# Queries of batches 1 to 3 loaded once and doubled by GpSimd, and outputs of batch 0 turned by DMA in two fp16 parts

## The chip, the core and the metric

One core of a Trainium2 chip runs the whole program. The metric is device time in microseconds, the median of three runs. The engines are named as in the profile: PE (TensorE; PEld is its weight load), DVE (VectorE), ACT (ScalarE), POOL (GpSimd) and SP (SyncE, which only issues DMAs here). Memory on the core is SBUF, with 128 partitions, and PSUM, into which PE writes.

## What is computed

```python
# q, k, v: (4 batches, 8 heads, 768, 64) f32; blocks of 32 rows, 24 of them
scores = q @ k.T / 8        # kept where |block_i - block_j| <= 1, in the first and last
                            # block row or column, or in 3 sampled blocks per row
attn = softmax(where(mask, scores, -1e9))
x = (attn @ v)              # heads side by side: (3072 tokens, 512)
out = ((x @ w_a) * (x @ w_b)) @ w_out       # w_a, w_b 512 x 1536, w_out 1536 x 512
```

## The kernel before

Queries go by **chunks** of 256 rows: 3 per batch, 12 in all, in the order 1, 0, 2, 3, ... 11. A chunk has 8 **units** (one block row of 32 queries, all 8 heads). For each unit GpSimd copies the keys it needs side by side (`KG`, lines 731 to 740), SP gathers the values from memory (`VG`, lines 821 to 835), PE makes scores (`s`), ACT the exponentials (`sm`), and PE the products with the values (`av`). Two units share one bank of `av`; `output` divides both by their sums (tile `xs`), turns them so that features lie on partitions, and writes them as two fp16 parts, high and low, to `xT`. Four such pairs make the chunk's `xT`, on which the feed-forward layer runs: 12 steps of 24 matmuls `ab` (line 1497), a product (`g`, lines 1513 and 1516), and the matmuls `o` (lines 1581 to 1583).

Batch 0 is computed in f32 straight from the inputs. Its pairs (12 of them) are turned on PE by two f32 matmuls with a unit matrix (line 1448), and ACT and DVE read the turned sums from PSUM and write the two parts (lines 1459 and 1460). Batches 1 to 3 run in two fp16 parts everywhere; their pairs (36) are split in SBUF (tile `xo`, lines 1433 and 1434) and turned by a transposing DMA that SP issues (line 1436).

The queries of batches 1 to 3 (9 chunks) come with both halves of the partitions holding the same 64 features, since the contraction runs over the keys' high part on one half and their low part on the other. The array in memory holds them twice. `queries` loads a chunk in two halves of 4 heads (line 865, 512 KB each, issued by POOL) into one buffer `rq` of 4 KB per partition; `half_queries` takes the largest absolute value (ACT, line 895), makes a scale from it (`set_scale`: one reduction over partitions on POOL, line 447, and three short DVE instructions), and writes the high part (ACT, line 901) and the low part (DVE, line 902). The second half's load waits until the first half's low part is done.

During the first third of the program the weights arrive as 64-bit words (36 tiles of 512 KB, line 951), are put together by DVE (lines 972 to 978), scaled and split by ACT and DVE (lines 992 to 1000).

The order of the instructions on each engine is worked out before the program runs: `Plan.run` takes generators ("flows"), each of which yields an engine, a duration in ns and a function that issues the instruction, and issues next the one that could begin first by its estimate, with the flow's rank to decide between equals. Each engine then runs its list in order. `LEAD_Q` sets the rank of the query flows; `GATE_Q` is how many units ahead of a chunk its queries may be asked for, and the two buffers `QT` must be free too. `LATE_...` is added to an estimated landing before the work that reads the data may be planned: 2500 ns (`LATE_XT`) for the turned outputs of batches 1 to 3.

Of the kernel before, what the change touches and what calls it, by code (L numbers as in the profile page):

```python
# [46 lines left out]
PT_BUFS = 3  # L47
SM_BUFS = 3
LATE = 16
RAW_PLACES = 2  # L50
EVEN = 0
AT_ONCE = 4
# [17 lines left out]

LEAD_K = 6
LEAD_V = 5
LEAD_Q = 4
LEAD_X = -1
LEAD_G = 2
GATE_KV = 10
GATE_Q = 9
GATE_Q0 = 6
GATE_G = 3
R_W = 12  # L80
# [186 lines left out]
def pe(ns, fn):  # L267
    return [Way("PE", ns, fn)]


def dve(ns, fn):
    return [Way("DVE", ns, fn)]


def act(ns, fn):
    return [Way("ACT", ns, fn)]
# [11 lines left out]
def pool_load(moved, fn):  # L288

    return [Way("POOL", 1000, fn, moved, 1000)]  # L290
# [7 lines left out]
def kernel(  # L298
# [43 lines left out]
    def take(tag, bufs):  # L342
        return rings.setdefault(tag, Ring(bufs)).take()
# [507 lines left out]
    def queries(cc):  # L851

        b, c = divmod(cc, NCH)
        u0 = order[b, c * PER]
        yield from gate(u0 - (GATE_Q if b else GATE_Q0))
        if b == 0:
            yield from plain_queries(cc, u0)
            return
        q_used[cc] = yield from take("QT", QT_BUFS)
        QT[cc] = work.tile([P, 2, H, CH], F16, tag="QT", name=f"QT{cc}", bufs=QT_BUFS)  # L860
        known = Event(2)
        for half in range(2):
            freed = yield from take("rq", 1)
            t = work.tile([P, NG, CH], F32, tag="rq", name=f"q{cc}_{half}", bufs=1)
            end = yield pool_load(2000, lambda t=t, half=half: nc.gpsimd.dma_start(
                t, q[b, c, :, half * NG : (half + 1) * NG]
            ))
            plan.start(half_queries(cc, half, t, freed, known), u0 - LEAD_Q, end + LATE_LOAD)
        next_queries(cc)
        yield k_scale[b]  # L870
        yield known

        def factor():

            for i in range(2):
                ps = slice(i * 64, (i + 1) * 64)
                nc.vector.scalar_tensor_tensor(
                    cq[ps, cc, :],
                    rscale[ps, at_k + b * NG : at_k + (b + 1) * NG].rearrange(
                        "p (a i) -> p a i", i=2  # L880
                    )[:, :, i],
                    float(D) ** -0.5, rscale[ps, at_q + 2 * cc : at_q + 2 * cc + 2],
                    ALU.mult, ALU.mult,
                )

        end = yield dve(450, factor)
        q_ready[cc].fire(end)

    def half_queries(cc, half, t, freed, known):
        b, c = divmod(cc, NCH)  # L890
        u0 = order[b, c * PER]
        at = at_q + 2 * cc + half
        heads = slice(half * NG, (half + 1) * NG)
        high, low_ = QT[cc][:, 0, heads], QT[cc][:, 1, heads]
        yield act(1230, lambda: nc.scalar.activation(
            high, t, AF.Abs, accum_out=bound[:, at : at + 1]
        ))
        end = yield from set_scale(slice(at, at + 1), FLOOR_QK)
        known.fire(end)
        s = scale[:, at : at + 1]  # L900
        yield act(1120, lambda: nc.scalar.activation(high, t, AF.Copy, scale=s))
        end = yield dve(1250, lambda: nc.vector.scalar_tensor_tensor(
            low_, t, s, high, ALU.mult, ALU.subtract
        ))
        freed.fire(end)
        q_ready[cc].fire(end)

    def next_queries(cc):
# [492 lines left out]
    def output(b, i, bank, read):  # L1401

        cc = b * NCH + i // PER
        p = place[cc]
        if p >= X_BUFS:
            yield ffn_done[seq[p - X_BUFS]]
        to = xT[p % X_BUFS][:, i % PER // 2]
        at = order[b, i] % LATE
        xs = work.tile([P, 2, HQ, D], F32, tag="xs", name=f"xs{b}_{i}", bufs=XS_BUFS)
        held = yield from take("xs", XS_BUFS)  # L1410
        dn = den[:, at : at + 2, :, 0]
        over = dn.unsqueeze(3).to_broadcast([P, 2, HQ, D])
        if b == 0:
            yield dve(165, lambda: nc.vector.tensor_scalar(dn, dn, EPS, None, ALU.add))
        else:
            yield v_scale[b]
            yield dve(165, lambda: nc.vector.scalar_tensor_tensor(
                dn, dn, EPS, evened[:, b].unsqueeze(1).to_broadcast([P, 2, HQ]),
                ALU.add, ALU.mult,
            ))  # L1420
        yield dve(160, lambda: nc.vector.reciprocal(dn, dn))
        sums = bank.rearrange("p y (i a d) -> p y i a d", i=2, a=HQ)
        if b == 0:
            yield dve(418, lambda: nc.vector.tensor_mul(xs, sums[:, 0], over))
        else:
            yield act(470, lambda: nc.scalar.copy(xs, sums[:, 1]))
            t = yield dve(418, lambda: nc.vector.tensor_add(xs, xs, sums[:, 0]))
            read.fire(t + LATE_AV)
            yield dve(430, lambda: nc.vector.tensor_mul(xs, xs, over))
            gone = yield from take("xo", XO_BUFS)  # L1430
            xo = work.tile([P, 2, 2, P], F16, tag="xo", name=f"xo{b}_{i}", bufs=XO_BUFS)
            flat = xs.rearrange("p i a d -> p i (a d)")
            yield act(400, lambda: nc.scalar.copy(xo[:, 0], flat))
            t = yield dve(420, lambda: nc.vector.tensor_sub(xo[:, 1], flat, xo[:, 0]))
            held.fire(t)
            t = yield sp(900, 760, lambda: nc.sync.dma_start_transpose(
                to.rearrange("p a x k q -> p (a x) (k q)"), xo.rearrange("p a i c -> p (a i c)")
            ))
            gone.fire(t + LATE_XO)
            x_ready[cc].fire(t + LATE_XT)  # L1440
            x_ready[cc].fire(t + LATE_XT)
            return
        ps = bank[:, 1].rearrange("p (i c) -> p i c", i=2)
        yield LATE_X if b else LATE_X0

        def turns_():
            for x in range(2):
                nc.tensor.transpose(
                    ps[:, x], xs[:, x].rearrange("p a d -> p (a d)"), eye
                )  # L1450

        t = yield pe(280, turns_)
        held.fire(t)
        if b == 0:
            yield v_scale[0]
        s = scale[:, at_v : at_v + 1] if b == 0 else 1.0
        of = ps.rearrange("p i c -> p (i c)")
        hi, lo = (to[:, a].rearrange("p x k q -> p (x k q)") for a in range(2))
        yield act(470, lambda: nc.scalar.activation(hi, of, AF.Copy, scale=s))
        t = yield dve(420, lambda: nc.vector.scalar_tensor_tensor(  # L1460
            lo, of, s, hi, ALU.mult, ALU.subtract
        ))
        read.fire(t + (LATE_AV if b else 0))
        x_ready[cc].fire(t)
        x_ready[cc].fire(t)


    gates, g_free = {}, {}
# [254 lines left out]
```

## Time and profile before

| | |
|---|---|
| median of 3 runs | 802.25 us (799.92 to 805.12) |
| the profiled execution's own time | 809.73 us |
| its span, first to last instruction | 807.6 us |
| granted PE clock, mean over the span | 0.976 |
| PE, PEld busy | 739.6 us (92%), 529.0 us (66%) |
| DVE, ACT, POOL busy | 522.0 us (65%), 492.0 us (61%), 228.4 us (28%) |
| DMA, whole span | 133.76 MB, 166 GB/s |

Busy time counts instructions that run; an engine that stands in front of a wait is idle. "DMA share" is the mean busy share of the core's 16 DMA engines. The clock is 1.00 at PE's upper level.

### The profile page before, as it was taken

Reading aid. Unit: us, or ns where it says so; the run is one execution under the profiler, and the core shown is the slowest. Engines: PE = TensorE matmul, PEld = TensorE weight load, DVE = VectorE, ACT = ScalarE, POOL = GpSimd, SP = SyncE. Lnnn points to the kernel's source line nnn. Section 1 sums busy time; section 2 is a strip of 40 time slices with the busy share of each in tenths; the row PEclk is TensorE's granted clock in tenths of the full one; section 3 lists DMA queues with packets and bytes.
Section 4 is the critical chain, followed back from the end, with each engine's and each line's share of the span. In section 5 each row is a group of like instructions: output and inputs, shape, how many; then the busy total and the mean of one; then the engine's idle time right before and its main releaser. Section 6 shows DMA issues by size and latency. Waiting matters only on the chain.

```text
span 807.6 us, 25925 instructions
## 1 busy us (share of the span) xinstructions
PE 739.6 (92%) x10056; PEld 529.0 (66%) x10056; DVE 522.0 (65%) x1478; ACT 492.0 (61%) x1226; POOL 228.4 (28%) x542
## 2 busy tenths in 40 slices
PE   2759979989989999899799999899899999999997
PEld 0426757864568767648568768558478768678853
DVE  4699979876766767575667676665666675622132
ACT  2767878875655776566556686666457565533333
POOL 4728743213233342121133332221133220000001
PEclk9968999999999999999999999999899999999999
DMA  9898667767687999885686799996688567630001
GB/s 271 239 285 246 204 212 241 217 126 178 146 181 164 198 139 224 184 208 144 154 177 170 167 194 194 184 241 133 147 180 175 137 141 148 137 83 1 2 0 53
DMA packets 185318, 133.76 MB, mean 166 GB/s; under 512 B 135851, under 2 KB 155948, under 8 KB 185196
## 3 DMA queue, kind: packets, MB, share of 16 engines
q1 hardware_dynamic: 172044, 84.85, 51.6%
q0 software_dynamic: 11616, 44.05, 18.1%
q10 hardware_dynamic: 1536, 3.21, 1.2%
q8 instruction: 79, 1.29, 0.7%
q14 instruction: 43, 0.35, 0.1%
HBM read 89.59 MB, written 11.01 MB: 125 GB/s over the span
## 4 chain that ended last, share of the span: by engine, by line
PE 69%; DMA 12%; DVE 8%; ACT 5%; issue 4%; SPq 1%; POOL 1%; POOLq 1%; ACTq 0%; DVEq 0%
PE ab L1497 39%; PE o L1581 7%; PE o L1583 6%; PE o L1582 6%; PE av L1094 4%; PE s L1035 4%; DMA pt<-hl 4%; DMA VG<-in_v_dram 2%; DMA stage<-in_v_dram 1%; DMA vp<-in_v_dram 1%; DMA q<-in_q_dram 1%; DMA keysT<-in_moe_w_b_dram 1%; SPq L835 1%; DMA keysT<-in_k_dram 1%; DVE wab L1000 1%
## 5 line engine op out<-in xcount | busy, mean ns | idle before, releaser
L1497 PE MATMUL ab<-xT,wab 128*128 128x256 f16 x3456 | 393.7, 275 | 7.6 <-ACT pt L1147 4.4
L1497 PEld LDWEIGHTS <-wab 128*128 128x128 f16 x3456 | 336.4, 99 | 61.0 <-issue 15.3
L1516 DVE TENSOR_TENSOR g<-g,ab 128x256 f32<-128x256 f32 x144 | 60.4, 419 | 119.2 <-ACT g L1513 118.5
L1513 ACT ACTIVATE g<-ab,f 128x256 f32<-128x256 f32 x144 | 67.9, 472 | 100.3 <-PE ab L1497 99.6
L1550 ACT ACTIVATE gh<-g,scale 128x256 f16<-128x256 f32 x144 | 70.9, 505 | 81.1 <-PE o L1583 76.1
L1551 DVE SCALAR_TENSOR_TENSOR gh<-g,scale,gh 128x256 f16<-128x256 f32 x144 | 68.3, 485 | 72.9 <-ACT gh L1550 71.8
L1581 PE MATMUL o<-wo,gh 128*128 128x512 f16 x288 | 110.7, 384 | 1.8 <-ACT gh L1550 1.8
L1582 PE MATMUL o<-wo,gh 128*128 128x512 f16 x288 | 110.2, 383 | 0.0
L1583 PE MATMUL o<-wo,gh 128*128 128x512 f16 x288 | 110.2, 382 | 0.0
L731 POOL COPY KG<-keysT 128x384 int32<-128x384 int32 (+1 forms) x86 | 50.0, 582 | 171.6 <-PE s L1035 144.1
L740 POOL COPY KG<-keysT 128x128 int32 (+1 forms) x264 | 88.5, 373 | 34.2 <-POOL KG L731 23.3
L1198 ACT ACTIVATE sm<-s,low,cq 128x256 f32<-128x256 f32 x132 | 73.9, 563 | 27.2 <-DVE low L1192 16.5
L447 POOL PARTITION_ALL_REDUCE power<-bound x67 | 28.9, 432 | 201.3 <-DVE bound L1530 82.4
L1061 DVE SCALAR_TENSOR_TENSOR hl<-sm,hl 128x256 f16<-128x256 f32 (+1 forms) x156 | 68.9, 452 | 1.6
L1186 DVE TENSOR_REDUCE low<-s 128x2 f32<-128x512 f32 x88 | 59.8, 680 | 6.8 <-PE s L1035 4.8
L1094 PE MATMUL av<-VG,pt 128*32 128x64 f32 (+2 forms) x2160 | 42.2, 218 | 24.0 <-DMA pt<-hl 9.7
L1581 PEld LDWEIGHTS <-gh 128*128 128x128 f16 x288 | 28.3, 98 | 37.7 <-issue 5.0
L1583 PEld LDWEIGHTS <-gh 128*128 128x128 f16 x288 | 28.4, 98 | 34.9 <-issue 1.1
L1582 PEld LDWEIGHTS <-gh 128*128 128x128 f16 x288 | 28.4, 99 | 30.5 <-issue 1.1
L1094 PEld LDWEIGHTS <-pt 128*32 128x32 f16 x2032 | 26.5, 97 | 27.0 <-DMA pt<-hl 16.3
L1520 ACT ACTIVATE junk<-g 128x1024 f16<-128x1024 f32 x36 | 37.9, 1053 | 9.9 <-DVE g L1516 9.3
L1035 PE MATMUL s<-KG,QT 128*32 128x256 f16 x1056 | 40.3, 273 | 0.0
(142 smaller groups left out, 946.4 us busy)
## 6 DMA issues: line engine op xcount, KB each, us to landing
VG<-vd SPq DMA_DIRECT2D x147, 64.0 KB, 2.8
q<-in_q_dram POOLq DMA_DIRECT2D x18, 512.0 KB, 5.6
VG<-vd SPq DMA_DIRECT2D x45, 192.0 KB, 3.4
out_dram<-ou POOLq DMA_DIRECT2D x24, 256.0 KB, 4.3
VG<-vd SPq DMA_DIRECT2D x15, 384.0 KB, 3.7
stage<-in_v_dram POOLq DMA_DIRECT2D x12, 384.0 KB, 5.2
vd<-vs SPq DMA_DIRECT2D x12, 384.0 KB, 5.3
stage<-in_k_dram POOLq DMA_DIRECT2D x12, 384.0 KB, 5.6
```

Of the source, the lines that this page charges most:

```text
L740: nc.gpsimd.tensor_copy(to[:, :, (5 + r) * w : (6 + r) * w], of[:, :, bass.ds(at, w)])
L1035: mm(to[h * BLK : (h + 1) * BLK], q_block(cc, i, 4 * hq + h, a), rhs(4 * hq + h), start=(first and a == 0), stop=(a == 1), skip_group_chec ...
L1061: t = yield dve(221 + n * 1.03, lambda: nc.vector.scalar_tensor_tensor(lo, sm, over, hi, ALU.mult, ALU.subtract))
L1094: mm(both[hs, :, i % 2, hq] if two else av[hs, i % 2, hq], pt[:, y, hs], of if two or b == 0 else of[:, 0], start=(i % 2 == 0 and hq == 0 ...
L1198: t = yield act(750, lambda hq=hq: nc.scalar.activation(sm[:, hq], ps[:, hq], AF.Exp, bias=low[:, at, hq, 0:1], scale=factor_of(b, cc, hq) ...
L1497: mm(ab[:, i, :].rearrange("p (j x q) -> p j x q", j=PER // 2, x=2), wab[:, f, i, part, kt, :], xc[:, :, a, :, kt, :], start=(i == 0 and k ...
L1513: yield act(460, lambda: nc.scalar.activation(g, ab[:, 0, :], AF.Copy, scale=f1[:, f : f + 1]))
L1550: yield act(400, lambda: nc.scalar.activation(gh[:, 0], g, AF.Copy, scale=s))
L1551: t = yield dve(480, lambda: nc.vector.scalar_tensor_tensor(gh[:, 1], g, s, gh[:, 0], ALU.mult, ALU.subtract))
L1581: mm(po, gh[:, 0, js], wo[:, x, 0], start=(x == 0), stop=False)
L1582: mm(po, gh[:, 0, js], wo[:, x, 1], start=False, stop=False)
L1583: mm(po, gh[:, 1, js], wo[:, x, 0], start=False, stop=(x == NF - 1))
```

## The change

The constants first: `LATE_XT0 = 1000` is new, `LEAD_Q` goes from 4 to 6, `GATE_Q` from 9 to 12.

**Queries.** A chunk's buffer now holds the first 4 heads on partitions 0 to 63 and the last 4 on 64 to 127, so that two loads of 64 partitions bring each number once (256 KB each), one after the other and without a wait between them. One absolute maximum and one scale serve the whole chunk. High and low part are written for 64 partitions at a time, and then a GpSimd copy brings both parts of those 4 heads to the other half of the partitions.

**Outputs of batch 0.** The two matmuls with the unit matrix, and the reads from PSUM, go. The divided sums are split in SBUF with the values' scale, into `xo`, and turned by the same transposing DMA that batches 1 to 3 use; the bank of `av` is given back right after the division.

```diff
         q_used[cc] = yield from take("QT", QT_BUFS)
         QT[cc] = work.tile([P, 2, H, CH], F16, tag="QT", name=f"QT{cc}", bufs=QT_BUFS)
-        known = Event(2)
-        for half in range(2):
-            freed = yield from take("rq", 1)
-            t = work.tile([P, NG, CH], F32, tag="rq", name=f"q{cc}_{half}", bufs=1)
-            end = yield pool_load(2000, lambda t=t, half=half: nc.gpsimd.dma_start(
-                t, q[b, c, :, half * NG : (half + 1) * NG]
+        known = Event()
+        freed = yield from take("rq", 1)
+        t = work.tile([P, NG, CH], F32, tag="rq", name=f"q{cc}", bufs=1)
+        for y in range(2):
+            ps = slice(y * D, (y + 1) * D)
+            end = yield pool_load(1000, lambda ps=ps, y=y: nc.gpsimd.dma_start(
+                t[ps], q[b, c, ps, y * NG : (y + 1) * NG]
             ))
-            plan.start(half_queries(cc, half, t, freed, known), u0 - LEAD_Q, end + LATE_LOAD)
+        plan.start(split_queries(cc, t, freed, known), u0 - LEAD_Q, end + LATE_LOAD)
         next_queries(cc)
         yield k_scale[b]
         yield known
@@ -879,30 +881,50 @@
                     rscale[ps, at_k + b * NG : at_k + (b + 1) * NG].rearrange(
                         "p (a i) -> p a i", i=2
                     )[:, :, i],
-                    float(D) ** -0.5, rscale[ps, at_q + 2 * cc : at_q + 2 * cc + 2],
+                    float(D) ** -0.5, rscale[ps, at_q + 2 * cc : at_q + 2 * cc + 1].to_broadcast([64, HQ]),
                     ALU.mult, ALU.mult,
                 )
 
         end = yield dve(450, factor)
         q_ready[cc].fire(end)
 
-    def half_queries(cc, half, t, freed, known):
-        b, c = divmod(cc, NCH)
-        u0 = order[b, c * PER]
-        at = at_q + 2 * cc + half
-        heads = slice(half * NG, (half + 1) * NG)
-        high, low_ = QT[cc][:, 0, heads], QT[cc][:, 1, heads]
+    def split_queries(cc, t, freed, known):
+        at = at_q + 2 * cc
+        to = QT[cc]
         yield act(1230, lambda: nc.scalar.activation(
-            high, t, AF.Abs, accum_out=bound[:, at : at + 1]
+            to[:, 0, :NG], t, AF.Abs, accum_out=bound[:, at : at + 1]
         ))
         end = yield from set_scale(slice(at, at + 1), FLOOR_QK)
         known.fire(end)
-        s = scale[:, at : at + 1]
-        yield act(1120, lambda: nc.scalar.activation(high, t, AF.Copy, scale=s))
-        end = yield dve(1250, lambda: nc.vector.scalar_tensor_tensor(
-            low_, t, s, high, ALU.mult, ALU.subtract
-        ))
+
+        def part(y):
+            ps, heads = slice(y * D, (y + 1) * D), slice(y * NG, (y + 1) * NG)
+            return ps, to[ps, 0, heads], to[ps, 1, heads], scale[ps, at : at + 1]
+
+        def high(y):
+            ps, hi, lo, s = part(y)
+            nc.scalar.activation(hi, t[ps], AF.Copy, scale=s)
+
+        def low_(y):
+            ps, hi, lo, s = part(y)
+            nc.vector.scalar_tensor_tensor(lo, t[ps], s, hi, ALU.mult, ALU.subtract)
+
+        def other(y):
+            ps, heads = slice(y * D, (y + 1) * D), slice(y * NG, (y + 1) * NG)
+            qs = slice((1 - y) * D, (2 - y) * D)
+            nc.gpsimd.tensor_copy(
+                to[qs, :, heads].rearrange("p a h q -> p a (h q)").bitcast(I32),
+                to[ps, :, heads].rearrange("p a h q -> p a (h q)").bitcast(I32),
+            )
+
+        for y in range(2):
+            yield act(1120, lambda y=y: high(y))
+            end = yield dve(1250, lambda y=y: low_(y))
+            plan.start(doubled(cc, lambda y=y: other(y)), order[cc // NCH, cc % NCH * PER] - LEAD_Q, end)
         freed.fire(end)
+
+    def doubled(cc, fn):
+        end = yield pool(1350, fn)
         q_ready[cc].fire(end)
 
     def next_queries(cc):
```

```diff
         yield dve(160, lambda: nc.vector.reciprocal(dn, dn))
         sums = bank.rearrange("p y (i a d) -> p y i a d", i=2, a=HQ)
         if b == 0:
-            yield dve(418, lambda: nc.vector.tensor_mul(xs, sums[:, 0], over))
+            t = yield dve(418, lambda: nc.vector.tensor_mul(xs, sums[:, 0], over))
+            read.fire(t)
         else:
             yield act(470, lambda: nc.scalar.copy(xs, sums[:, 1]))
             t = yield dve(418, lambda: nc.vector.tensor_add(xs, xs, sums[:, 0]))
             read.fire(t + LATE_AV)
             yield dve(430, lambda: nc.vector.tensor_mul(xs, xs, over))
-            gone = yield from take("xo", XO_BUFS)
-            xo = work.tile([P, 2, 2, P], F16, tag="xo", name=f"xo{b}_{i}", bufs=XO_BUFS)
-            flat = xs.rearrange("p i a d -> p i (a d)")
+        gone = yield from take("xo", XO_BUFS)
+        xo = work.tile([P, 2, 2, P], F16, tag="xo", name=f"xo{b}_{i}", bufs=XO_BUFS)
+        flat = xs.rearrange("p i a d -> p i (a d)")
+        if b == 0:
+            yield v_scale[0]
+            s = scale[:, at_v : at_v + 1]
+            yield act(400, lambda: nc.scalar.activation(xo[:, 0], flat, AF.Copy, scale=s))
+            t = yield dve(480, lambda: nc.vector.scalar_tensor_tensor(
+                xo[:, 1], flat, s, xo[:, 0], ALU.mult, ALU.subtract
+            ))
+        else:
             yield act(400, lambda: nc.scalar.copy(xo[:, 0], flat))
             t = yield dve(420, lambda: nc.vector.tensor_sub(xo[:, 1], flat, xo[:, 0]))
-            held.fire(t)
-            t = yield sp(900, 760, lambda: nc.sync.dma_start_transpose(
-                to.rearrange("p a x k q -> p (a x) (k q)"), xo.rearrange("p a i c -> p (a i c)")
-            ))
-            gone.fire(t + LATE_XO)
-            x_ready[cc].fire(t + LATE_XT)
-            x_ready[cc].fire(t + LATE_XT)
-            return
-        ps = bank[:, 1].rearrange("p (i c) -> p i c", i=2)
-        yield LATE_X if b else LATE_X0
-
-        def turns_():
-            for x in range(2):
-                nc.tensor.transpose(
-                    ps[:, x], xs[:, x].rearrange("p a d -> p (a d)"), eye
-                )
-
-        t = yield pe(280, turns_)
         held.fire(t)
-        if b == 0:
-            yield v_scale[0]
-        s = scale[:, at_v : at_v + 1] if b == 0 else 1.0
-        of = ps.rearrange("p i c -> p (i c)")
-        hi, lo = (to[:, a].rearrange("p x k q -> p (x k q)") for a in range(2))
-        yield act(470, lambda: nc.scalar.activation(hi, of, AF.Copy, scale=s))
-        t = yield dve(420, lambda: nc.vector.scalar_tensor_tensor(
-            lo, of, s, hi, ALU.mult, ALU.subtract
-        ))
-        read.fire(t + (LATE_AV if b else 0))
-        x_ready[cc].fire(t)
-        x_ready[cc].fire(t)
+        t = yield sp(900, 760, lambda: nc.sync.dma_start_transpose(
+            to.rearrange("p a x k q -> p (a x) (k q)"), xo.rearrange("p a i c -> p (a i c)")
+        ))
+        gone.fire(t + LATE_XO)
+        late = LATE_XT if b else LATE_XT0
+        x_ready[cc].fire(t + late)
+        x_ready[cc].fire(t + late)
 
 
     gates, g_free = {}, {}
```

## Rows read from the trace of the kernel before

**Rows 1.** The page, part 1: busy us, share, instructions.
```profile
PE 739.6 (92%) x10056; PEld 529.0 (66%) x10056; DVE 522.0 (65%) x1478; ACT 492.0 (61%) x1226; POOL 228.4 (28%) x542
```
**Rows 2.** Stretches: start:end, length, busy us per engine, clock, DMA.
```profile
core 0: us, PE busy (x) PEld busy (x) DVE busy (x) ACT busy (x) POOL busy (x), PEclk, DMA share, GB/s
20.00:60.00 40.00, 26.91 (x420) 14.76 (x421) 31.68 (x75) 27.05 (x86) 19.77 (x43) 0.82 0.94 263
60.00:116.00 56.00, 50.06 (x848) 36.68 (x848) 54.31 (x130) 46.34 (x132) 38.27 (x70) 0.95 0.76 229
116.00:720.00 604.00, 575.92 (x8135) 415.94 (x8135) 405.17 (x1185) 383.48 (x943) 158.62 (x399) 0.99 0.79 172
300.00:350.00 50.00, 44.35 (x622) 33.00 (x614) 31.34 (x96) 30.79 (x72) 10.24 (x29) 0.97 0.99 199
500.00:550.00 50.00, 46.31 (x612) 31.55 (x610) 33.58 (x104) 31.25 (x72) 10.88 (x28) 1.00 0.94 189
```
**Rows 3.** Chain that ended last: start us, us, what.
```profile
101.05 8.13 DMA keysT<-in_moe_w_b_dram
...
116.32 4.45 PE ab L1497 x24
...
180.21 1.04 ACT QT L895 x2
```
**Rows 4.** Waits of TensorE: total us, times, longest.
```profile
PE av L1094 <- DMA pt<-hl: 13.2, 9, 3.3
...
PE av L1094 <- ACT pt L1147: 7.3, 5, 2.5
...
PE av L1094 <- DMA VG<-in_v_dram: 6.0, 5, 1.9
```
**Rows 5.** Stretches, line 1448 alone; and their sum.
```profile
0.00:60.00 60.00, 1.51 (x6) 0.74 (x6) 0.88 0.93 266
...
116.00:808.00 692.00, 1.58 (x8) 0.95 (x8) 0.99 0.70 152
sum 808.00, PE 5.11 PEld 2.84; mean PE 1.70 PEld 0.95
```
**Rows 6.** Timeline of TensorE: start, us, what.
```profile
68.17 0.38 PE L1448 MATMUL av<-eye,xs 128*128 128x128 f32 x2
...
68.48 0.54 PE L1094 MATMUL av<-vp,pt 128*32 128x64 f32 x24
...
71.99 2.79 PE L1497 MATMUL ab<-xT,wab 128*128 128x256 f16 x24
```
**Rows 7.** Tile xo: ns min/median/max, first and last start.
```profile
L1434 DVE TENSOR_TENSOR xo<-xs,xo x36: 410/419/724, 226.2 to 723.4; 128x256 f16<-128x256 f32 x36
L1436 SPq DMA_TRANSPOSE xT<-xo x36: 1188/1207/2937, 228.5 to 723.9; - x36
...
DMA to landing us min/median/max: 2.4/4.0/7.2
```
**Rows 8.** The page, part 3: queue, packets, MB, share.
```profile
q1 hardware_dynamic: 172044, 84.85, 51.6%
q0 software_dynamic: 11616, 44.05, 18.1%
```
**Rows 9.** Tile QT: ns min/median/max.
```profile
L895 ACT ACTIVATE QT<-q x18: 1039/1049/1061, 111.7 to 617.9; 128x1024 f16<-128x1024 f32 x18
L895 ACT ACTIVATION_READ_ACCUMULATOR QT<-q x18: 185/190/205, 112.6 to 618.9; 128x1 f32 x18
L902 DVE SCALAR_TENSOR_TENSOR QT<-q,scale,QT x18: 1254/1283/1378, 134.0 to 626.8; 128x1024 f16<-128x1024 f32 x18
```
**Rows 10.** GpSimd by line: ns min/median/max; its longest wait.
```profile
L731 POOL COPY KG<-keysT x86: 498/511/1522, 14.7 to 672.7; 128x384 int32<-128x384 int32 x66, 128x384 f32<-128x384 f32 x20
L740 POOL COPY KG<-keysT x264: 288/297/1509, 11.7 to 674.4; 128x128 int32 x99, 128x128 f32 x33
...
POOL KG L731 <- PE s L1035: 144.1, 34, 14.2
```

More of the change, by code (lines that the diff above doesn't have):

```diff
@@ L49 @@
 LATE = 16
+LATE_XT0 = 1000
 RAW_PLACES = 2
@@ L72 @@
 LEAD_V = 5
-LEAD_Q = 4
+LEAD_Q = 6
 LEAD_X = -1
@@ L76 @@
 GATE_KV = 10
-GATE_Q = 9
+GATE_Q = 12
 GATE_Q0 = 6
```

## The prediction

> **What bounds the kernel now.** I read the page's busy times first. PE is at work for 739.6 of 807.6 us, no other engine for more than 65% [rows 1], so what is taken from another engine counts only where PE stands still for it. The stretches say where that is. In 60 to 116 us DVE is busy for 54.31 of 56 us while PE has 50.06 and a clock of 0.95; from 116 to 720 us PE has 575.92 of 604 us at 0.99 and no other engine is above 68% [rows 2]. The chain of waits agrees: it passes through the weights' arrival at 101.05 us and the first stretch of feed-forward matmuls after it at 116.32 us [rows 3]. So there are three regimes. Up to 60 us memory sets the pace (DMA share 0.94 in 20 to 60 us), up to 116 us it is DVE's unpacking of weights, and then PE, which up to 720 us stands still for 604 - 575.92 = 28.1 us in all. That is all that better feeding of PE could win there; beyond it only PE's own work can shrink. The waits name the largest piece of it: 13.2 us in front of the products with the values, for the turned exponentials' DMA [rows 4]. Two stretches hold much of the rest: 300 to 350 us (5.65 us idle, DMA share 0.99) and 500 to 550 us (3.69 us, 0.94) [rows 2].
>
> **Turns off PE.** 24 matmuls with their weight loads go, 5.11 us of PE in all [rows 5]. Those before 116 us win nothing by themselves: PE was not the bound there. The 8 after it (4 pairs) are 1.58 us busy. A pair really takes 68.48 - 68.17 = 0.31 us of PE's time, as the next matmul shows [rows 6]. So 4 x 0.31 = 1.2 us, on the path: **-1.2 us**. Ends: 0 (a stall behind takes it up) and -5.1 (all 24 count).
>
> **The parts of batch 0's outputs.** The 12 ACT and 12 DVE instructions that write the parts stay in number; DVE's takes 0.419 us in later batches [rows 7]. Both its inputs are now in SBUF; the longest such case took 0.724 us [rows 7], so at most 12 x 0.305 = 3.7 us more of DVE. Of the 12 pairs 3 fall before 60 and 4 after 116 us [rows 5], so 5 lie in DVE's own stretch: 1.5 us if every one is held. I take 0, the median's case, and keep 0 and +3.7 as ends.
>
> **The turn by DMA.** Added: 12 transposing DMAs on SP, 1.2 us of issue each, landing 2.4 to 7.2 us after it, 4.0 in the median [rows 7]. This takes the place of a 0.31 us turn. Chunk 1's last turn was at 68.17 us and its first feed-forward step at 71.99 us [rows 6]; the split was in between anyway, so the data now come later by 4.0 - 0.3 = 3.7 us in the median and 6.9 us at worst. PE has units of attention to do meanwhile, if the written order puts them first: the order counts with 1 us after its own estimate of the landing (2.5 us for later batches), so it knows most of this. I take **+1 us**, for one of three chunks a third of the median; ends 0 and +11 (three chunks by 3.7). The transposes wait on SP for DVE's low part; behind them on SP are the gathers of values, for which PE waits: 6.0 us in five places already, in the memory-bound start [rows 4]. A transpose is 131 KB. Queue q1 took 0.516 x 807.6 = 417 us for 84.85 MB [rows 8], 4.9 us per MB, so 0.64 us each, 7.7 us of DMA time for 12. The 3 pairs before 60 us make 1.9 us there; half of it on the path: **+1 us**, ends 0 and +3.6 (3 x 1.2 us of SP).
>
> **Queries.** Bytes: 18 loads of 0.524 MB become 18 of half that, 4.72 MB less. Queue q0 took 0.181 x 807.6 = 146 us for 44.05 MB [rows 8], 3.3 us per MB: 15.6 us of DMA time less, against 7.7 us more above. In the two full stretches (300 to 350 and 500 to 550 us) one load each of 0.524 x 3.3 = 1.7 us less lies in front of what PE waits for: **-3.5 us**. Ends: 0 (the loads were hidden) and -13.2 (the whole wait).
> ACT: 9 times 1.049 + 0.190 us less [rows 9], 11.2 us. ACT is nowhere the bound, with one place excepted: the chain passes through the queries' absolute value at 180.21 us [rows 3], behind which ACT reads the turned exponentials that PE waits for (7.3 us in 5 places [rows 4]). One instruction less there: **-1.2 us**, ends 0 and -2.5 (two).
> High and low parts: 18 instructions each before and after, over 64 partitions instead of 128 and as many elements in each, so 1.28 us on DVE as before [rows 9]: 0.
> POOL: 9 reductions less, 18 copies more. No row shows a copy to other partitions. Of those in place, 128 columns took 0.297 and 384 took 0.511 us [rows 10], 0.84 ns per column, so 1024 columns take 0.511 + 640 x 0.00084 = 1.05 us; the slowest 384-column copy took 1.522 us, three times the median, which gives 3.1 us as the upper end. That is 18 x 1.05 = 18.9 us more of POOL, up to 56. POOL's longest wait is for PE to be done with a unit's keys, 144.1 us [rows 10], and this idle time covers it. Each copy waits for DVE's low part, and behind it on POOL stand the key copies, for which PE's scores wait. They have two buffers and 1.6 us of work (0.511 + 3 x 0.297) per unit. Units follow each other by (720 - 200) / 72 = 7.2 us, so a copy can be some 5 us late before PE notices. Cost 0, ends -1 (POOL no longer waits for the buffer in front of a chunk's second load) and +4 (one such delay in each of batches 1 to 3, by 1.3 us). That the copy comes before the chunk can start adds 1 or 3 us to a preparation that begins some 8 units, 58 us, ahead: 0.
>
> **Sum.** -1.2 + 1 + 1 - 3.5 - 1.2 = -3.9 us. Against the profiled execution's 809.73 us that is 805.8; that execution is 7.5 us over the median of the three runs (and over the longest), so I carry the difference to the median: 802.25 - 3.9 = 798.35, say **798.5 us**.
>
> **A page against it.** On POOL beside DVE the rows show copies of one size from 0.498 to 1.522 us [rows 10] and DVE instructions with two inputs in SBUF from 0.410 to 0.724 us [rows 7]: each at times stands in the other's way. The Trainium skill, SBUF — State Buffer, "Who interferes with whom", has the rule for it: a DVE instruction with two SBUF inputs and a GpSimd instruction that reads SBUF exclude each other for their whole length. The spread agrees with that.
>
> **Rivals.** (a) *Copies hold DVE.* The 18 new copies read SBUF, and DVE's splits have two inputs there. If each holds up one split by 0.305 us (0.724 - 0.419) and PE feels all of it, +5.5 us: 804. For it the spread above; against it that DVE has a third of its time free after 116 us [rows 2]. Chance 0.08.
> (b) *Nothing on the path.* Loads were hidden, the turns' 1.2 us go into the next wait: 802. For it PE's 28.1 us idle, of which no single wait depends on queries. 0.12.
> (c) *The stalls close.* With ACT 11 us and DMA some 8 us lighter, and the banks of batch 0 given back at once, the rewritten order loses half of the 28.1 us on top of the turns less what (d) costs: about -12, 790. For it that the worst idle stretches have a DMA share of 0.94 to 0.99 [rows 2]; against it that queries are 9.4 of q0's 44 MB [rows 8] and q1 is the busier queue. 0.30.
> (d) *The first batch's features come late.* Where the sum has 1 us, PE stands in front of the feed-forward steps of chunks 1, 0 and 2 for 3.7 to 6.9 us each, and DVE behind PE, so that the weights slip too: 798.4 - 1 + 3 x 4.9 = 812. It decides from about 4.3 us a chunk (810.3). For it that landing, 4 us in the median, was measured mostly with a DMA share of 0.79, and it is 0.94 in the start; against it that the order was written knowing of the DMA. 0.18.
> My forecast has the remaining 0.32.
>
> **Range and chances.** A change of 1% (8 us) is about what can be told from none here, the three runs spreading over 0.65%. Forecast, (a) and (b) lie within 1% (794.2 to 810.3): 0.52. Faster is (c), 0.30, slower (d), 0.18. For 8 in 10 the range takes the unknown ends of the middle cases, (c) down to 788 and (d) up to 812.
>
> **What would show it.** In the changed profile: no line-1448 matmuls and PE's busy time less by about 5 us; 48 turned outputs; q0 with some 4.7 MB less; 18 copies on POOL of 1.0 to 1.4 us; nine reductions and ACT maxima fewer. The steps are right if PE's idle time from 116 to 720 us falls from 28 to about 24 us and its waits for turned exponentials shrink at 300 to 350 and 500 to 550 us. They are wrong if the feed-forward's first step stands clearly later than 72 us with a wait for the turned outputs before it (d), if DVE's two-input instructions spread wider and PE waits for DVE (a), or if PE waits for key copies with a doubling in front of them on POOL. A reordering that moves whole stretches would make the small terms meaningless in either direction.

## The result: 1.4% slower

The changed kernel took 815.02 us in the median of 6 runs (810.69 to 817.91), the kernel before 803.57 us on the same chip (799.92 to 808.14): a ratio of 1.014 with the interval 1.0102 to 1.0179 (95%). Ratios here and below come from executions of the two kernels on the same chip, without those that fell in the chip's slower state, so they need not be the quotient of the medians. I had forecast 798.5 us, in a range of 788 to 812.

The profiled execution of before took 809.73 us, over its median; that of the changed kernel took 810.69 us, the fastest of its six. The two traces hide the difference, so each kernel was traced once more: before at 801.33 us (span 799.2), the change at 813.01 us (span 810.8). Below, "before" is that second trace, and the changed kernel is shown by its first (span 808.4).

**The operations came as forecast.** The changed kernel's page, parts 1 and 3, in the columns of [rows 1, 8]:

```profile
PE 738.3 (91%) x10032; PEld 525.4 (65%) x10032; DVE 523.0 (65%) x1446; ACT 485.1 (60%) x1213; POOL 249.3 (31%) x551
...
q1 hardware_dynamic: 178572, 86.43, 53.6%
q0 software_dynamic: 10464, 39.33, 16.4%
```

24 matmuls fewer, 4.72 MB fewer on q0, 20.9 us more of POOL. Its tiles QT and xo (ns min/median/max, first and last start), against [rows 7, 9]:

```profile
L906 ACT ACTIVATE QT<-q,scale x18: 1132/1144/1157, 117.0 to 612.0; 64x1024 f16<-64x1024 f32 x18
L910 DVE SCALAR_TENSOR_TENSOR QT<-q,scale,QT x18: 1255/1284/1609, 118.6 to 616.0; 64x1024 f16<-64x1024 f32 x18
L915 POOL COPY QT<-QT x18: 1032/1037/1632, 121.6 to 619.1; 64x1024 int32<-64x1024 int32 x18
...
L1467 SPq DMA_TRANSPOSE xT<-xo x48: 1188/1215/2620, 30.1 to 724.6; - x48
L1465 DVE TENSOR_TENSOR xo<-xs,xo x36: 406/418/726, 236.5 to 724.1; 128x256 f16<-128x256 f32 x36
...
L1460 DVE SCALAR_TENSOR_TENSOR xo<-xs,scale,xo x12: 473/486/592, 29.3 to 197.0; 128x256 f16<-128x256 f32 x12
...
DMA to landing us min/median/max: 2.4/4.5/9.5
```

A GpSimd copy takes 1.037 us where I estimated 1.05. Most of DVE's two-input instructions spread no wider than before (`xo`: 0.726 us at most, 0.724 before), but two groups do: the low parts of the queries (1.609 us at most, 1.378 before) and the short factors `low` (1.028 us, 0.504 before).

**Where the time went.** Stretches (start:end, length, busy us per engine, clock, DMA share, GB/s), the changed kernel and then before:

```profile
60.00:116.00 56.00, 48.50 (x800) 34.64 (x793) 53.08 (x128) 46.54 (x131) 40.41 (x70) 0.91 0.96 245
116.00:200.00 84.00, 74.50 (x844) 54.18 (x843) 65.01 (x173) 61.75 (x140) 21.77 (x38) 0.96 0.69 182
200.00:300.00 100.00, 94.09 (x1381) 62.63 (x1380) 67.19 (x190) 59.61 (x154) 36.63 (x92) 0.98 0.72 155
...
sum 720.00, PE 655.04 PEld 464.88 DVE 499.92 ACT 454.31 POOL 246.41; mean PE 81.88 PEld 58.11 DVE 62.49 ACT 56.79 POOL 30.80
```

```profile
60.00:116.00 56.00, 49.31 (x848) 36.49 (x848) 54.17 (x127) 45.99 (x131) 36.99 (x70) 0.96 0.76 227
116.00:200.00 84.00, 77.77 (x934) 56.46 (x933) 66.15 (x180) 64.72 (x153) 23.49 (x50) 0.94 0.67 186
200.00:300.00 100.00, 97.71 (x1440) 68.19 (x1439) 72.05 (x212) 63.08 (x160) 35.11 (x87) 1.00 0.83 169
...
sum 720.00, PE 665.20 PEld 477.18 DVE 502.43 ACT 464.12 POOL 224.44; mean PE 83.15 PEld 59.65 DVE 62.80 ACT 58.02 POOL 28.06
```

The last line of each sums the eight stretches up to 720 us. PE stands idle there for 720 - 655.04 = 65.0 us in the changed kernel and for 54.8 us before. These 10.2 us cover the 9.2 us between the spans, and 6.9 of them lie between 116 and 300 us (9.5 + 5.9 against 6.2 + 2.3). DVE and ACT have no more work there than before. The whole sum varies from one execution to the next: in the first trace of before PE idles for 63.0 us up to 720 us, and in the second trace of the changed kernel for 63.0 us too. The stretch from 116 to 300 us is steadier: 15.4 and 15.9 us in the two traces of the changed kernel, 10.2 and 8.5 us in the two of before. So some 5 to 7 us of the loss are placed there, and the rest isn't placed. PE's waits over the whole span (us, times, longest), the changed kernel and then before:

```profile
PE av L1116 <- ACT pt L1169: 9.4, 8, 2.6
PE o L1589 <- ACT gh L1558: 8.3, 2, 5.3
...
PE av L1116 <- DMA pt<-hl: 2.8, 3, 1.6
```

```profile
PE av L1094 <- ACT pt L1147: 5.7, 5, 2.5
PE av L1094 <- DMA pt<-hl: 4.8, 5, 1.9
...
PE o L1581 <- ACT gh L1550: 2.0, 1, 2.0
```

PE now waits for ACT's and DVE's short pieces, for the features' two parts (`gh`) above all. The wait for turned exponentials, 13.2 us in [rows 4], was 4.8 us in the second trace of before.

**The longest of these waits, 5.3 us, read closely.** Changed kernel, timelines of DVE, POOL, ACT and PE (start, us, what, idle before it and its releaser):

```profile
257.87 1.37 DVE L910 SCALAR_TENSOR_TENSOR QT<-q,scale,QT 64x1024 f16<-64x1024 f32 x1
...
263.00 1.28 DVE L910 SCALAR_TENSOR_TENSOR QT<-q,scale,QT 64x1024 f16<-64x1024 f32 x1
...
265.65 0.24 DVE L1214 TENSOR_TENSOR low<-low,cq 128x2 f32<-128x2 f32 x1
...
266.75 0.99 DVE L1214 TENSOR_TENSOR low<-low,cq 128x2 f32<-128x2 f32 x1
...
266.42 1.31 POOL L915 COPY QT<-QT 64x1024 int32<-64x1024 int32 x1
...
265.93 0.56 ACT L1220 ACTIVATE sm<-s,low,cq 128x256 f32<-128x256 f32 x1 [2.82 <-DVE low L1214]
...
270.58 1.31 ACT L1558 ACTIVATE gh<-g,scale 128x256 f16<-128x256 f32 x3
...
263.08 2.79 PE L1505 MATMUL ab<-xT,wab 128*128 128x256 f16 x24
271.15 0.61 PE L1589 MATMUL o<-wo,gh 128*128 128x512 f16 x1 [5.27 <-ACT gh L1558]
```

Both low parts of one chunk stand 5.1 us apart on DVE, with the two high parts on ACT before them. Behind the second stand the row maxima, their factors (`low`), and the last product of the features (`g`). ACT waits for DVE for 2.82 us, `gh` begins at 270.58, PE stands for 5.27 us. The second low part holds DVE for 1.28 us of this, and the long factor takes 0.75 us more than the one before it.

The rest is the order on PE itself. In the changed kernel `o`, which needs `gh`, stands right behind the 24 `ab` that end at 265.9. In before PE has attention and 48 more `ab` to do from 268.4 us on, while the same short steps run, and comes to `o` at 275.7:

```profile
269.70 2.79 PE L1497 MATMUL ab<-xT,wab 128*128 128x256 f16 x24
...
273.06 2.79 PE L1497 MATMUL ab<-xT,wab 128*128 128x256 f16 x24
275.69 0.38 PE L1581 MATMUL o<-wo,gh 128*128 128x512 f16 x1
```

In 250 to 275 us before and the changed kernel read:

```profile
250.00:275.00 25.00, 25.00 (x430) 21.57 (x419) 19.46 (x62) 16.84 (x42) 11.06 (x29) 1.00 0.84 181
```

```profile
250.00:275.00 25.00, 19.73 (x396) 15.40 (x398) 18.87 (x52) 16.28 (x40) 8.72 (x20) 0.93 0.65 143
```

Before has two halves of a chunk there too, as much DVE and ACT work, and a PE that never stops. Its halves are 15.5 us apart (252.18 and 267.72): the single buffer `rq` let the second load start only when the first half was split. The changed kernel holds a chunk in one buffer, and all nine chunks have their two low parts 4 to 5 us apart (the first 11), where before has 14 to 21 us.

### The profile page after: what moved, and what is told of

Same layout as the page of the kernel before. It is cut to its first block, busy times and chain, and to the rows that moved or that the text cites. A ratio compares the mean times of both kernels' runs of the same rounds, so it can differ in the third digit from the quotient of the medians.

```text
span 808.4 us, 25868 instructions
## 1 busy us (share of the span) xinstructions
PE 738.3 (91%) x10032; PEld 525.4 (65%) x10032; DVE 523.0 (65%) x1446; ACT 485.1 (60%) x1213; POOL 249.3 (31%) x551
## 4 chain that ended last, share of the span: by engine, by line
PE 59%; issue 11%; DMA 10%; DVE 8%; ACT 6%; POOL 2%; SPq 1%; POOLq 1%; ACTq 0%; DVEq 0%
PE ab L1505 32%; PE o L1589 6%; PE o L1591 5%; PE o L1590 5%; PE av L1116 4%; PE s L1057 3%; DMA stage<-in_v_dram 3%; PE s L1048 2%; ACT sm L1220 1%; DMA VG<-vd 1%; DMA keysT<-in_moe_w_a_dram 1%; DVE QT L910 1%; DMA stage<-in_moe_w_a_dram 1%; DMA vp<-in_v_dram 1%; PE tp L1164 1%
## 5 line engine op out<-in xcount | busy, mean ns | idle before, releaser
L1589 PE MATMUL o<-wo,gh 128*128 128x512 f16 x288 | 111.9, 389 | 8.3 <-ACT gh L1558 8.3
L1591 PE MATMUL o<-wo,gh 128*128 128x512 f16 x288 | 111.5, 387 | 0.0
L1590 PE MATMUL o<-wo,gh 128*128 128x512 f16 x288 | 111.3, 387 | 0.0
L741 POOL COPY KG<-keysT 128x128 int32 (+1 forms) x264 | 91.6, 384 | 32.8 <-POOL KG L732 16.6
L448 POOL PARTITION_ALL_REDUCE power<-bound x58 | 27.2, 469 | 199.5 <-DVE bound L1538 93.8
L1528 ACT ACTIVATE junk<-g 128x1024 f16<-128x1024 f32 x36 | 37.9, 1054 | 10.8 <-DVE g L1524 10.8
L1637 POOL DMA_DIRECT2D out_dram<-ou x24 | 13.3, 554 | 86.7 <-ACT ou L1635 84.8
```

The lines of the kernel that those rows point to most:

```text
L741: nc.gpsimd.tensor_copy(to[:, :, (5 + r) * w : (6 + r) * w], of[:, :, bass.ds(at, w)])
L1589: mm(po, gh[:, 0, js], wo[:, x, 0], start=(x == 0), stop=False)
L1590: mm(po, gh[:, 0, js], wo[:, x, 1], start=False, stop=False)
L1591: mm(po, gh[:, 1, js], wo[:, x, 0], start=False, stop=(x == NF - 1))
```

## The experiments

All ratios are to the kernel before on the same chip. A run's own median stands first.

**The parts, each in an order of its own.** e1 has only the queries' part, with both constants (`LEAD_Q` 6, `GATE_Q` 12); e2 only the outputs' part; e3 only the two constants:

```diff
-LEAD_Q = 4
+LEAD_Q = 6
-GATE_Q = 9
+GATE_Q = 12
```

> The queries' part alone, with its two constants; outputs of batch 0 as before. If the loss of 11 us comes with the queries (GpSimd's copies, or the order that their flows bring), this is 808 to 816 us. If it comes with the outputs, it is within 4 us of before, 800 to 807. If only the order counts, whichever edit causes it, both this and the outputs alone may be anywhere from -5 to +12 us, and the two need not add up to 11.

> The outputs' part alone, with its constant; queries as before. If the turn by DMA in the memory-bound start is the cost, 810 to 818 us, with PE's idle time and lower clock before 140 us as in the changed kernel. If the queries are, 800 to 806. If the order, anywhere from -5 to +12 us.

> The kernel before with the change's two constants for queries alone (rank 6 for 4, gate 12 for 9 units): no operation is added or taken away, only the written order of the engines differs. If the order by itself moves the time by the size of the loss, this differs from before by 4 us or more, either way (795 or less, or 805 or more). If the operations set it, 799 to 803 us.

e1: 806.69, 1.0037 (1.0000 to 1.0075). e2: **798.89, 0.9930 (0.9886 to 0.9975)**. e3: **819.0, 1.0238 (1.0201 to 1.0276)**. Not one part adds up with another: e1 and e2 together would be a gain of 0.3%, and e3, in which no operation is added or taken away, loses more than the whole change. e3's lists of instructions part from before's at some 105 us, and from there the order differs on every engine. `Plan.run` also chooses for each high part of the exponentials (`hl`) whether ACT or DVE makes it: in e3 it gave 16 of 48 from ACT to DVE. That isn't the cause by itself, since e14 below gives 2 of them the other way and loses 2.0%. `GATE_Q` alone changes no instruction's place, in before and in the changed kernel alike, so the rank alone did it. e3's sum up to 720 us:

```profile
sum 720.00, PE 651.68 PEld 463.44 DVE 499.21 ACT 453.96 POOL 226.03; mean PE 81.46 PEld 57.93 DVE 62.40 ACT 56.75 POOL 28.25
```

PE idles for 68.3 us against 54.8, with the operations of before; the mean granted clock is 0.970 against 0.974.

**The operations, without the new order.** e6 puts the outputs' operations, e7 the queries', into before's lists: the added instruction is issued within the step that makes its data, and nothing else moves. e10 has both parts' operations (with a maximum and scale per half, so nine more of each than the change) in e2's order, the copies issued as in e7.

```diff
# e7, e10 (e6 the same with the transposing DMA, at the step of the outputs' low part)
-        end = yield dve(1250, lambda: nc.vector.scalar_tensor_tensor(
-            low_, t, s, high, ALU.mult, ALU.subtract
-        ))
+        def low_and_double():
+            nc.vector.scalar_tensor_tensor(low_, t, s, high, ALU.mult, ALU.subtract)
+            nc.gpsimd.tensor_copy(
...
+        end = yield dve(1250, low_and_double)
```

> The outputs' operations of the change in the order of before: every engine's list is the one of before, except that the 24 matmuls with the unit matrix are gone, the parts are written in SBUF, and SP's transposing DMA stands where DVE's low part is issued. If the operations cost (DMA in the start, gathers behind the transposes), 808 to 816 us. If the order is the cost, 799 to 805: the turns' 1 to 4 us of PE won, less a wait of up to 3 us for the first feed-forward step, which is now not planned for.

> The queries' operations in the order of before: each half is loaded once, on its 64 partitions, with a maximum and a scale of its own as before, and GpSimd's copy to the other partitions is put into POOL's list where DVE's low part is issued. No other instruction moves. If GpSimd's 18 copies (1.0 to 1.6 us each) hold up DVE or the key copies, 807 to 815 us, with waits of PE for key copies. If they are hidden, 800 to 805.

> All operations of the change in the order of the outputs alone (which took 798.9 us): the queries' halves are loaded once, split on 64 partitions and doubled by GpSimd, with a maximum and a scale per half as before, and nothing else moves. If the order that the queries' flows bring is the cost, 799 to 806 us (the same edit cost 3.8 us in the order of before). If the operations of the two parts cost when together, 811 to 819 us like the changed kernel.

e7: 804.53, 1.0017 (0.9982 to 1.0052): the copies are hidden, and the smaller loads gain nothing. e10: **803.54, 1.0001 (0.9970 to 1.0033)**: everything the change computes, for nothing. e6: 809.34, 1.0066 (1.0024 to 1.0108), which is in the range that was expected if the operations cost: in before's order the outputs' part does cost 0.7%, and in its own (e2) it gains as much. In e6 the order knows of no landing, and here the late features of rival (d) are seen, in one place; e6's waits in 55 to 125 us and PE's timeline:

```profile
PE ab L1495 <- DMA xT<-xo: 10.8, 2, 9.3
```

```profile
68.95 1.04 PE L1026 MATMUL s<-KG,QZ 128*32 128x256 f32 x16
79.28 2.96 PE L1495 MATMUL ab<-xT,wab 128*128 128x256 f16 x13 [9.29 <-DMA xT<-xo]
```

The changed kernel, whose order counts with the landing, has none of it; its first feed-forward step comes at 70.56 us, 1.4 us earlier than in [rows 6]:

```profile
69.60 1.03 PE L1048 MATMUL s<-KG,QZ 128*32 128x256 f32 x16
70.56 2.68 PE L1505 MATMUL ab<-xT,wab 128*128 128x256 f16 x23
```

**The whole change again, and with the old constants.**

> The changed kernel once more, beside the others on one chip, for a second trace. Both theories: 811 to 819 us, 1.0 to 1.8% over before.

> The changed kernel with the two constants of before (rank 4, gate 9): the same operations in another order. If the order is the cost, it moves by 4 us or more from the changed kernel's 815, most likely down towards the 803 that the two parts measured alone add up to. If the operations are, it stays within 811 to 819 us.

e9: 814.18, 1.0173 (1.0134 to 1.0211). e4 (rank 4): 810.58, 1.0120 (1.0081 to 1.0159). The rank is worth some 4 us here, though the two intervals overlap; 1.2% stay with the rank of before.

**Other ranks.** Before once more as it is (e13), with rank 5 (e14) and 3 (e15); the changed kernel with 5 (e16) and 2 (e19). Each is one number in `LEAD_Q`.

> The kernel before once more, for a trace of an execution nearer to its median: the one shown took 809.7 us. If the 9 us between that one and the median are in the first 200 us, its PE loses less there; if they are in 300 to 400 and 500 to 600 us, the waits for the turned exponentials' DMA (13.2 us) are shorter here and the term of -3.5 us for them had nothing to win in the median execution. Time 799 to 805 us.

> The kernel before with rank 5 for 4 for the queries' flows, no operation changed. If earlier queries cost by a mechanism of their own (they take ACT's, DVE's and POOL's turns from the weights and the values), this lies between rank 4 (801) and rank 6 (819), at 806 to 814 us. If any other order is as good as a draw, it may be anywhere from 795 to 820 us, out of line with 4 and 6.

> The kernel before with rank 3 for 4 for the queries' flows, no operation changed. If earlier queries cost by a mechanism, later ones do not: 795 to 803 us. If the order is a draw, and the order of before a lucky one, 803 to 818 us here too.

> The changed kernel with rank 5 for 6 for the queries' flows, no operation changed. Rank 4 took 810.6 and rank 6 814 to 815 us. By the mechanism 811 to 814 us; by the draw anywhere from 797 to 818 us, and a time under 806 us would show that the change's operations do not need more than before's.

> The changed kernel with rank 2: queries give way to the units in flight on every engine. If going ahead of them is the cost, 801 to 809 us, less than rank 4's 810.6. If rank 4 and 6 differ only by the draw of an order, anywhere from 800 to 818 us.

e13: one execution, 801.33. e14: 818.28, 1.0196 (1.0147 to 1.0245). e15: 801.33, 1.0015 (0.9982 to 1.0048). e16: 811.16, 1.0121 (1.0075 to 1.0168). e19: **823.68, 1.0250 (1.0199 to 1.0300)**. Before has a step between 4 and 5 and no more than 0.4% on either side. In the changed kernel rank 2 is the slowest of all, outside both ranges that were expected: that a smaller rank is better as such fell with it.

**The halves apart again.** The flow that splits a chunk rests by plan before its second half: 10 us (e17), 6 us (e21) or 14 us (e22) with rank 4, and 10 us with the change's rank 6 (e18). No operation changes.

```diff
         for y in range(2):
+            if y:
+                yield 10000
             yield act(1120, lambda y=y: high(y))
```

> The changed kernel with rank 4 and a planned pause of 10 us between a chunk's two halves (before, the single buffer kept them 13 to 18 us apart on DVE; in the changed kernel they are 4 to 5 us apart). If the bunching of the two halves is what is left of the loss at rank 4, 801 to 806 us, as all operations of the change took in the outputs' order (803.5). If not, 808 to 813 us as without the pause (810.6).

> The changed kernel, rank 6, with the same pause of 10 us between the halves. If the bunching is the cost and the rank is not, 801 to 807 us. If the rank is, 811 to 817 us as without the pause (814 to 815). In between if both share it.

> The changed kernel with rank 4 and a pause of 6 us for 10. If keeping the halves apart is what counts, and not the one lucky order that 10 us gave, 800 to 807 us, or between 802 and 811 if 6 us is too little. If every order is a draw, anywhere from 800 to 824 us, the span of the orders so far.

> The same with 14 us. If keeping the halves apart counts, 800 to 806 us, as with 10 us (801.9). If every order is a draw, anywhere from 800 to 824 us.

With rank 4: 6 us 803.59, 1.0034 (1.0004 to 1.0064); 10 us **801.88, 0.9994 (0.9961 to 1.0027)**; 14 us 803.08, 1.0025 (0.9987 to 1.0063). Without a pause it was 1.0120 (e4). Three orders with the halves apart (8 to 26 us on DVE) agree within 0.4%, and all lie 0.8% or more under e4. With rank 6: 808.65, 1.0081 (1.0049 to 1.0113), against 1.014 and 1.0173 without the pause. e4 and then e17, 250 to 275 us and the sum up to 720 us:

```profile
250.00:275.00 25.00, 19.89 (x420) 15.30 (x418) 19.46 (x53) 14.44 (x36) 12.55 (x29) 0.93 0.84 152
...
sum 720.00, PE 652.62 PEld 465.29 DVE 504.09 ACT 456.49 POOL 241.03; mean PE 81.58 PEld 58.16 DVE 63.01 ACT 57.06 POOL 30.13
```

```profile
250.00:275.00 25.00, 25.00 (x475) 21.86 (x474) 19.90 (x60) 16.82 (x43) 11.40 (x23) 1.00 0.66 149
...
sum 720.00, PE 661.59 PEld 474.35 DVE 503.86 ACT 455.77 POOL 244.01; mean PE 82.70 PEld 59.29 DVE 62.98 ACT 56.97 POOL 30.50
```

The same stretch that PE lost 5 us in is full again, with the low parts at 256.23 and 269.37 us, and the 9.0 us of idle time less are the 9.0 us between the spans (808.2 and 799.2). So a pause wins the loss back at rank 4. That the halves' distance does it, and not the new order that comes with a pause, is likely but not shown: e20 below, rank 4 in another order with the halves still close, loses 1.9%. But e4's 5 us in this stretch aren't the wait read above: 4.5 of them are waits for turned exponentials, 0.6 for `gh`. e16 has the halves of that chunk 3.7 us apart, and PE works there nearly without a gap:

```profile
250.00:275.00 25.00, 24.68 (x400) 21.43 (x398) 18.79 (x57) 16.68 (x45) 9.65 (x25) 1.00 0.81 152
```

At rank 6 the pause takes the halves 13.6 us apart, and the long wait for `gh` is still there (e18):

```profile
264.67 1.45 DVE L910 SCALAR_TENSOR_TENSOR QT<-q,scale,QT 64x1024 f16<-64x1024 f32 x1
...
278.24 1.28 DVE L910 SCALAR_TENSOR_TENSOR QT<-q,scale,QT 64x1024 f16<-64x1024 f32 x1
...
268.86 0.61 PE L1591 MATMUL o<-wo,gh 128*128 128x512 f16 x1 [5.48 <-ACT gh L1560]
```

So that wait doesn't need two halves in one burst. e18's one trace has PE idle for 68.3 us, no less than the changed kernel's 65.0, and where its gain comes from isn't seen in it. Its granted clock is higher (0.981 against 0.976 and 0.967), but another execution of e18, at 0.973, took the same 808.6 us.

**A longer planned landing.** In the changed kernel with rank 4, `LATE_XT0` 2500 in place of 1000:

> The changed kernel with rank 4 and the landing of batch 0's turned outputs planned 2.5 us later instead of 1.0. If PE's losses in 60 to 200 us (24 to 26 us in the changed kernel, 18 to 19 before) come from turned outputs that land later than planned, this takes 3 us or more off 810.6: 803 to 808 us. If they come from the added DMA itself, 809 to 813 us.

e20: 818.56, 1.0192 (1.0135 to 1.0249). More time planned for the first batch's features cost some 0.7% over e4, outside both ranges that were expected, with the same operations in another order.

## Why the prediction was wrong

What decided is a step that the sum doesn't have: the **written order**. I priced each operation where it had stood, and named a moving of whole stretches only in the last sentence. e3 shows the order's price with no operation added (+2.4%), and e10 the operations' in another order (nothing).

- **The buffer.** I counted its loss as a gain ("POOL no longer waits for the buffer", down to -1 us). It was what kept a chunk's halves 14 to 21 us apart. With the halves together the changed kernel loses 1.2% at rank 4, and three pauses give back 0.9, 1.3 and 1.0%: this much is shown at rank 4. At rank 6 a pause gives back 0.6 to 0.9%. That the distance does it, and not the new order, is likely and not shown.
- **The constants.** I described them and gave them no price. `GATE_Q` does nothing. The rank costs +2.4% alone (e3, no operation added), about 4 us in the changed kernel without a pause (e4 to e9) and 7 us with it (e17 to e18).
- **"Turns off PE" (-1.2), "parts" (0), "turn by DMA" (+1 and +1).** Together +0.8 by the sum. They have no price of their own: e2 measured -0.7% (-1.1 to -0.3), that is -5.6 us, and e6, with the same operations in before's order, +0.7%. The matmuls went as counted. DVE's 12 low parts took 0.486 us for my 0.419, under 1 us in all. The DMA's size was too small. Queue q1's packets took 50.9% of 799.2 us in the second trace of before, 407 us, and 433 us in the changed kernel; over all traces it is 407 to 417 us with 36 transposes and 416 to 435 with 48. The means, 411 and 426 us, make 1.2 us for each of the 12 (an estimate), twice my 0.64. In 60 to 116 us, with 5 transposes, the DMA share is 0.96 in the changed kernel and 0.98 in e2, against 0.76 before and 0.74 in e7, which has the queries' part alone; but e16, with 5 too, has 0.87, so no price follows from that stretch. PE's waits for turned outputs are 10.8 us in e6, 7.3 in e19, and 2.6 to 3.6 in e2, e10, e4 and the three pauses at rank 4; the changed kernel has none.
- **"Queries" (-3.5 by DMA, -1.2 by ACT).** The bytes and the nine instructions went. e7, which has the smaller loads, shows what these were worth on the path: +0.2% (-0.2 to +0.5). It keeps 18 maxima, so no run prices ACT's nine fewer by themselves. The -3.5 was also twice what its own figures give: one load brings 0.262 MB less, which is 0.87 us at 3.3 us per MB, and 0.524 MB is the saving of a whole chunk. I read a wait of 13.2 us from one execution; in another it was 4.8 us.
- **"POOL" (0).** Right: 18 copies of 1.037 us, hidden (e7). A unit's key copies are 1.4 us (0.511 + 3 x 0.297) and not 1.6, which changes nothing.
- **Rival (a)** is seen inside the burst: beside the copy at 266.42 us the factors' multiplication took 0.99 us, and 0.24 us a microsecond before. The Trainium skill's rule (SBUF — State Buffer, "Who interferes with whom") agrees with that row, in which both end together, at 267.7 us. As a price of its own it didn't decide: such a multiplication took up to 0.984 us in e7 too, whose time can't be told from before's.
- **Rival (b)** was the truth about the operations in e2's order (e10, 1.0001); in before's the outputs' part costs 0.7% (e6). **Rival (c)** gave the new order half of PE's idle time; the order decided, with the other sign: PE's idle time from 116 to 720 us is 27.8 us (before 19.1), and not 24. **Rival (d)**'s 812 was near by its number only, since its wait is in e6 and not in the changed kernel.

**Open.** Why one order of the same operations is worth 1.2 to 2.5% less than another isn't shown. For the halves' distance: of ten orders of the changed kernel's operations, the five with the halves 3 to 9 us apart but for the first chunk (ranks 6, 5, 4 and 2, and e20) lose 1.2 to 2.5%, and the five with 8 to 27 us (the four pauses and e10) lose 0 to 0.8%. Against it as the whole cause: e1 has its halves 2.5 to 5.4 us apart and loses 0.4%, e3 and e14 have theirs 10 to 20 us apart and lose 2%. So the distance is likely to be part of it, by a path that the traces don't show. What rank 5 in before, rank 2 and the longer landing in the changed kernel did to which stretch was not told apart.

The best kernel of these is the outputs' part alone, e2: 0.9930 (0.9886 to 0.9975), faster than both.

## What to carry to other kernels

Where a program writes the order of the instructions, a rank or a buffer count is an edit with a price, and it can be larger than that of all operations: run the operations in the old order and the constants alone before crediting either. A single buffer also spaces work out; where one goes, look at what now arrives in one burst in front of short steps that the bounding engine waits for, and try spacing it by hand. Look too at what stands directly behind such steps in the bounding engine's own list: without other work there it waits for the whole chain. A wait read from one execution is worth what a second execution confirms.

## What the runs showed of the hardware

- Twelve transposing DMAs of 131 KB more (1.58 MB) added some 15 us to the time of q1's packets, 411 to 426 us in the mean of the traces: an estimate of 1.2 us each of all 16 engines, where the queue's mean rate gave 0.64.
- GpSimd's copy from 64 partitions to the other 64, 1024 columns, took 1.037 us in the median; the copies within their partitions gave 1.05 by their time per column [rows 10].
- A DVE multiplication of 128x2 numbers with both inputs in SBUF took 0.99 us beside such a copy, and 0.24 us a microsecond earlier.
- The same operations in other orders took from 801.9 us (e17) to 823.7 us (e19) in the changed kernel, and from 801.3 us (e15) to 819.0 us (e3) in before; up to 16 high parts of exponentials stand on DVE instead of ACT in some of them.
